# The products of an inverse 47-point unit, tied in issue order and begun on the second PSUM bank

## The chip, the cores and the metric

The kernel runs on one core of a Trainium2 chip. The metric is the device time of one execution in microseconds. Beside it stands a profile of one execution, taken on the chip. The engines are TensorE (PE, with its weight loads as PEld), VectorE (DVE), ScalarE (ACT), GpSimd (POOL) and SyncE (SP, which issues most DMAs).

## The reference

A filter along the sequence (a real Fourier transform, a complex mixing matrix, a soft threshold, the inverse transform) on 8 batches of 3008 positions and 256 channels, and behind it a gated feed-forward network (FFN) on all 24064 tokens:

```python
X = np.fft.rfft(x, axis=1)
Yr = Xr @ w_r - Xi @ w_i + b_r
Yi = Xr @ w_i + Xi @ w_r + b_i
Yr = np.sign(Yr) * np.maximum(np.abs(Yr) - lam, 0.0)   # the same for Yi
y = np.fft.irfft(Yr + 1j * Yi, n=x.shape[1], axis=1)
gate = 1.0 / (1.0 + np.exp(-(y @ w_gate)))
out = (gate * (y @ w_val)) @ w_out
```

## The kernel before

3008 is 47 · 64, so each transform is done as products with a table of 47 points (step a) and tables of 64 points (step b). The program has three parts. First the transforms of the first batches run in blocks whose order is the code's own (`tc.manual_schedule()`). Then the FFN of the first 9 · 512 tokens (`ffn1`, `ffn2`) runs together with the transforms of the other batches; here a scheduler decides the order on each engine: it goes by the order in the code and takes another instruction first where it expects that one to be ready sooner. From about 1021 us on, the remaining tokens go through the FFN in another algorithm, with an order that is written out by hand (`ORDER`, `slot`).

The change touches two helpers of step a.

`products_a` does the forward 47-point products: four products for a pair of PSUM banks `pa`, in the code's order second bank first.

`inv_a(u)` does the inverse ones for a unit `u` of 2 · 4 · 47 positions. Its input `vf` comes from DRAM in `load_v`, which `move` issues as two DMAs on SP: rows 0 to 47 first, rows 64 to 111 second. They belong to the two halves `j` of the unit. Each half is 16 products of 48 rows by 64 channels by 47 points (fp32), over four `h`, two `ct` and two `e`. The half decides which 64 rows of the array a product uses, and `e` which 64 columns: four quarters. Half `j` writes bank `pa[j]` (named `pia` in the profile; the program numbers its tiles, so the second bank of a unit has the higher number). Behind the products ACT copies both banks: to `yf`, which SP stores in DRAM (`yd`) for the last part, or to `yth`/`carry` for the FFN of the middle part. The banks come from a ring of 6 that `pg` and `pv` of the FFN use too; `vf` has 2 buffers, and a third tile for some units near the end.

The loop over `j` is in the middle, so the code goes two products on the first bank, two on the second, and so on. There are 64 units. Around each stand, on PE, the FFN's products `pg` and `pv` (L474 to L476, 12 of them) and `po` (L502 to L504, 6 of them). Sigmoid (L480), product (L482), split into `hh` and `hl` (L490, L491) of the FFN run on ACT and DVE.

`hook` is a list that is filled while the FFN runs in the blocks of fixed order, and is cleared behind them (`hook.clear()`).

Of the kernel before, what the change touches and what calls it, by code (L numbers as in the profile page):

```python
# [19 lines left out]
R2, R1 = 47, 64  # L20
# [101 lines left out]
def tile_fft_mix_ffn(ctx: ExitStack, tc, x, w_r, w_i, b_r, b_i, w_one, w_out, mf, mi, mis, fa, fb, mf0, fa0, out):  # L122
    nc = tc.nc
# [29 lines left out]
    def bank(name, tag="ring", bufs=RING):  # L153
        return (psf if tag == "ring" else psl).tile([P, 512], F32, tag=tag, bufs=bufs, name=name)
# [10 lines left out]
    fb_sb = const.tile([P, 64], F32, name="fb_sb")  # L165
# [3 lines left out]
    fa_sb = const.tile([P, 64], F32, name="fa_sb")  # L169
# [32 lines left out]
    def load_a(b, h):  # L202
# [4 lines left out]
            move(nc.sync, xf, xv[b, h])  # L207
        held["x", b, h] = xf

    def products_a(xs, outs, copies):  # L210
        pa = [bank("pa") for _ in range(2)]
        xs = [t[:, 2 * c:2 * c + 2] if t.shape[1] == 4 else t for c, t in enumerate(xs)]
        for j in (1, 0):
            rows = slice(64 * j, 64 * j + R2)
            for c in (1, 0):
                nc.tensor.matmul(pa[j][64 * c:64 * c + 64], fa_sb[rows], xs[c][rows], start=True, stop=True)
        for copy, o, t in zip(copies, outs, pa):
            copy(o, t.rearrange("p (h c) -> p h c", h=2))

    def fwd_a(b, h):  # L220

        xf = held["x", b, h]
        if b == 0:
            for i, copy in enumerate((nc.scalar.copy, nc.vector.tensor_copy)):
                pa, xi = bank("pa")[:2 * NQ], xf[:2 * NQ, 2 * i:2 * i + 2]
                nc.tensor.matmul(pa, fa0_sb, xi, start=True, stop=True)
                copy(xi, pa.rearrange("p (h c) -> p h c", h=2))
            return
        products_a((xf, xf), (xf[:, 0:2], xf[:, 2:4]), (nc.scalar.copy, nc.vector.tensor_copy if b < 2 else nc.scalar.copy))
# [13 lines left out]
    def halves_a(b, u):  # L243

        xs = [held.pop(("xh", b, 2 * u + c)) for c in range(2)]
        az = [p2.tile([P, 2, D], F32, tag="st", bufs=NST, name="azh") for _ in range(2)]
        products_a(xs, az, (nc.scalar.copy, nc.scalar.copy))
        for j in range(2):
            move(nc.gpsimd, az[j], zv[b][u, :, :, 2 * j:2 * j + 2], True)
# [144 lines left out]
    def split_y(c, at, n, y):  # L394
        if c not in yts:
            yts[c] = [p3.tile([P, CT, CW], F32R, name=t) for t in ("yth", "ytl")]
        yh, yl = (t[:, :, at:at + n] for t in yts[c])
        nc.scalar.copy(yh, y)
        sub(yl, y, yh)

    def inv_a(u):
        vf = held.pop(("v", u))
        pa = [bank("pia")[:, :CT * UT].rearrange("p (c k) -> p c k", c=CT) for _ in range(2)]
        for h in range(4):
            for ct in range(CT):
                for j in range(2):
                    rows = slice(64 * j, 64 * j + NQ)
                    for e in range(2):
                        ch = ct * P + 64 * e
                        nc.tensor.matmul(pa[j][64 * e:64 * e + 64, ct, h * R2:(h + 1) * R2], vf[rows, h, ch:ch + 64],  # L410
                                         fb_sb[rows, :R2], start=True, stop=True)
        first = 2 * u * UT // CW
        for j, py in enumerate(pa):
            lo, k = (2 * u + j) * UT, 0
            while k < UT:
                at = lo + k
                c, place = divmod(at, CW)
                n = UT - k if at >= T0 else min(UT - k, CW - place)
                y = py[:, :, k:k + n]
                if at >= T0:  # L420
                    t = result("yf")[:, :CT * n].rearrange("p (c k) -> p c k", c=CT)
                    nc.scalar.copy(t, y)
                    nc.sync.dma_start(yd[:, :, at - T0:at - T0 + n], t)
                elif c == first:
                    split_y(c, place, n, y)
                else:
                    if place == 0:
                        held["carry", c] = p3.tile([P, CT, 384], F32, name="carry", bufs=1), 0
                    t = held["carry", c][0]
                    nc.scalar.copy(t[:, :, place:place + n], y)  # L430
                    held["carry", c] = t, place + n
                k += n

    def result(name):
        return p3.tile([P, CW], F32, tag="ry", bufs=NYF, name=name)
# [11 lines left out]
    hook = []  # L447
# [111 lines left out]
    def ffn_units():  # L559
        units, todo = [], {}  # L560
        seq = [(c, f) for c in range(NPL) for f in range(NF)]

        def own(c):

            return range(-(-c * CW // (2 * UT)), -(-(c + 1) * CW // (2 * UT)))

        for c in range(1, NPL):
            at = (c - 1) * NF
            for i, u in enumerate(own(c)):
                todo.setdefault(at + (0, 4)[i], []).append(lambda u=u: load_v(u))  # L570
                todo.setdefault(at + (4, 8)[i], []).append(lambda u=u: inv_a(u))
            todo.setdefault(at + 1, []).append(lambda c=c: carry(c))

        def unit(n):
            c, f = seq[n]
            if n == 0:
                for i, u in enumerate(own(0)):
                    if i == 0:
                        w = w1h[:, 0].rearrange("p i t n -> p (i t n)")
                        keep_warm(bank("warm"), w[:, :P], w, WARM_V)  # L580
                    inv_a(u)
                ops("sum word", 0)
            ffn1(c, f)
            for t in todo.pop(n, ()):
                t()
            if n >= LAG and n - LAG < len(seq) - BEHIND:
                ffn2(*seq[n - LAG])
        return [lambda n=n: unit(n) for n in range(len(seq))], own(0), own(NPL - 1)[-1] + 1
# [61 lines left out]
    xs = {}  # L650
# [468 lines left out]
    def inverse(g):  # L1119

        us = [u for b in g for u in range(b * NV, (b + 1) * NV) if u >= u0]
        last = g == groups[-1]
        ahead = min(NVF - 1, len(us))
        todo = list(range(len(us)))

        def load(upto):
            while todo and todo[0] < upto:
                i = todo.pop(0)
                load_v(us[i], last and i > 4 and i % 3 == 2)

        def begin():
            load(ahead)

        def go(i):
            load(i + 1 + ahead + (last and i > 3))
            inv_a(us[i])
        return [(0.0, begin)], [(1.0, lambda i=i: go(i)) for i in range(len(us))]
# [32 lines left out]
    for j in range(NF, len(ffn)):  # L1170
        c, f = divmod(j, NF)
# [94 lines left out]
```

## Time and profile before

| what | before |
|---|---|
| median of 3 runs (lowest to highest) | 2664.31 us (2664.19 to 2669.71) |
| the profiled execution | 2665.18 us |
| its span, first to last instruction | 2663.2 us |
| granted TensorE clock, mean | 0.996 |
| PE busy | 2627.3 us (99%) |
| PEld busy | 2456.9 us (92%) |
| DVE, ACT, POOL busy | 1941.7, 1816.8, 1094.1 us |
| products of `pia` (records of PE) | 4096, from 99.8 to 1008.1 us |

A row of the timeline is the start in us, the time from the start to the end of the last instruction in it, the engine, the source line, the operation, what it writes and reads, the shape and the count; instructions of one kind that follow each other are one row. An fp32 product leaves two records, so a unit of `pia` counts x64. In brackets stands how long the engine was idle ahead of it, and what ended that.

### The profile page before, as it was taken

The numbers are of one execution on the slowest core, as the hardware profiler recorded it, in microseconds if no ns is written. First come the engines' busy times: TensorE is split into PE (matmuls) and PEld (weight loads), VectorE is DVE, ScalarE is ACT, GpSimd is POOL, SyncE is SP. The second block draws the span as 40 slices with busy tenths as digits, with TensorE's granted clock in tenths as the row PEclk, the third lists the DMA queues.
The fourth block names the chain that finished last, engine by engine and source line by source line (L and its number), as shares of the span: only waits on it lengthen the run. The fifth ranks groups of instructions, "written<-read, shape, count | busy, mean of one in ns | idle before, by whom it ended". The sixth has DMA issues, their size and how long they took to land. (4 is left out here: it accounts for less than half of the span.)

```text
span 2663.2 us, 60273 instructions
## 1 busy us (share of the span) xinstructions
PE 2627.3 (99%) x24032; PEld 2456.9 (92%) x24032; DVE 1941.7 (73%) x3468; ACT 1816.8 (68%) x3530; POOL 1094.1 (41%) x1399
## 2 busy tenths in 40 slices
PE   8999999999999999999999999999999999999998
PEld 6668888888899878999999999999999999999998
DVE  4768778777777525777777777777777777777777
ACT  4666655656565435777777777777777777777776
POOL 0241031123500002555555555555555555555554
PEclk9999999999999999999999999999999999999999
DMA  9887655777655572111111211111111211111111
GB/s 282 259 249 201 189 153 170 195 226 221 198 161 150 175 222 76 33 41 34 39 41 35 47 32 42 33 41 34 40 41 33 46 31 45 33 41 33 40 41 27
DMA packets 200969, 268.27 MB, mean 101 GB/s; under 512 B 19760, under 2 KB 152368, under 8 KB 200688
## 3 DMA queue, kind: packets, MB, share of 16 engines
q1 hardware_dynamic: 179600, 220.04, 28.1%
q0 software_dynamic: 20832, 44.31, 7.8%
q8 instruction: 189, 3.10, 0.5%
q14 instruction: 92, 0.75, 0.1%
q10 hardware_dynamic: 256, 0.07, 0.0%
HBM read 137.33 MB, written 127.01 MB: 99 GB/s over the span
## 5 line engine op out<-in xcount | busy, mean ns | idle before, releaser
L764 POOL TENSOR_TENSOR hs<-gh,xh 128x256 f32<-128x256 f32 x227 | 253.1, 1115 | 734.6 <-DVE gh L754 734.6
L754 DVE TENSOR_TENSOR gh<-gh,pa 128x256 f32<-128x256 f32 x228 | 96.1, 421 | 344.4 <-ACT gh L749 344.4
L713 PE MATMUL pd<-xop,th 128*128 128x256 f32 x1824 | 333.0, 276 | 0.8 <-DVE pc L757 0.8
L713 PE MATMUL pa<-xop,w1h 128*128 128x256 f32 x1824 | 332.6, 276 | 0.0
L713 PEld LDWEIGHTS pd<-xop,th 128*128 128x128 f32 x1824 | 274.5, 188 | 1.7 <-DVE pc L757 1.4
L713 PEld LDWEIGHTS pa<-xop,w1h 128*128 128x128 f32 x1824 | 274.6, 188 | 0.1
L713 PE MATMUL pd<-xop,tl 128*128 128x256 f32 x912 | 251.8, 276 | 0.0
L713 PE MATMUL pa<-xop,w1l 128*128 128x256 f32 x912 | 251.7, 276 | 0.0
L784 DVE TENSOR_TENSOR hpS<-hs,hpS 128x768 fp32r<-128x768 f32 x228 | 217.1, 952 | 0.4 <-ACT hpS L780 0.4
L733 ACT COPY pd<-pb 128x512 f32<-128x512 f32 x228 | 130.0, 570 | 107.8 <-PE pb L713 107.8
L757 DVE TENSOR_TENSOR pb<-pb,m 128x512 f32<-128x512 f32 x228 | 159.5, 699 | 42.3 <-PE pb L713 42.3
L327 PE MATMUL pm<-w_sb,xsh 128*128 128x256 f32 x1008 | 185.9, 286 | 4.1 <-ACT xsh L310 3.1
L780 ACT CAST hpS<-hs 128x768 fp32r<-128x768 f32 x228 | 189.5, 831 | 0.2 <-DVE hs L770 0.2
L729 PE MATMUL acc<-hpS,w2h 128*128 128x256 f32 x912 | 177.5, 276 | 0.0
L733 ACT COPY pb<-pa 128x512 f32<-128x512 f32 x228 | 130.0, 570 | 68.1 <-PE pa L713 68.0
L770 POOL TENSOR_TENSOR hs<-xh,hs 128x256 f32<-128x256 f32 x227 | 168.0, 740 | 17.8
L768 POOL TENSOR_TENSOR gh<-gh 128x256 f32<-128x256 f32 x227 | 167.3, 737 | 17.8
L713 PEld LDWEIGHTS pd<-xop,tl 128*128 128x128 f32 x912 | 171.2, 188 | 0.0
L713 PEld LDWEIGHTS pa<-xop,w1l 128*128 128x128 f32 x912 | 171.2, 188 | 0.0
L766 POOL TENSOR_TENSOR hs<-hs,gh 128x256 f32<-128x256 f32 x227 | 168.1, 741 | 0.0
L713 PE MATMUL pb<-xop,th 128*128 128x256 f32 x912 | 166.5, 276 | 0.0
L713 PE MATMUL pb<-xop,w1h 128*128 128x256 f32 x912 | 166.4, 276 | 0.0
(218 smaller groups left out, 8738.4 us busy)
## 6 DMA issues: line engine op xcount, KB each, us to landing
zf<-zd SPq DMA_DIRECT2D x96, 256.0 KB, 4.3
vf<-vd SPq DMA_DIRECT2D x128, 192.0 KB, 4.1
vd<-vz SPq DMA_DIRECT2D x85, 256.0 KB, 3.1
ypair<-yd SPq DMA_DIRECT2D x38, 512.0 KB, 3.6
yd<-yf SPq DMA_DIRECT2D x103, 188.0 KB, 3.8
out_dram<-ev SPq DMA_DIRECT2D x149, 128.0 KB, 1.8
out_dram<-ev POOLq DMA_DIRECT2D x37, 512.0 KB, 5.8
xf<-in_x_dram SPq DMA_DIRECT2D x80, 192.0 KB, 4.4
```

Source lines behind the costliest of these rows:

```text
L327: nc.tensor.matmul(o, l, r, start=(i == 0), stop=(i == len(mms) - 1))
L713: nc.tensor.matmul(o[:, i * HW:(i + 1) * HW], l, r, start=start, stop=l is wl, skip_group_check=True)
L729: nc.tensor.matmul(o, l, r, start=(p, b) not in begun, stop=l is wl, skip_group_check=True)
L733: nc.scalar.copy(to, o)
L754: nc.vector.tensor_mul(g, g, o[:, HW:])
L757: nc.vector.tensor_add(to, o, hx[k, "m5"])
L764: e.tensor_add(hx[k, "S"][:, 0], g[:, 1], x[:, 1])
L766: e.tensor_sub(hx[k, "S"][:, 1], hx[k, "S"][:, 0], g[:, 0])
L768: e.tensor_sub(g[:, 1], g[:, 0], g[:, 1])
L770: e.tensor_sub(hx[k, "S"][:, 2], x[:, 0], hx[k, "S"][:, 1])
L780: nc.scalar.copy(t[:, 0], parts_of(k, what))
L784: sub(t[:, 1], parts_of(k, what), t[:, 0])
```

## The change

A new helper `behind_last_of` ties each product to the instruction traced last on TensorE, from the second product of a unit on: the scheduler may not issue it ahead of that one. It is not a wait for the other to finish; it binds the order of issue alone, and other instructions may come between. In the blocks of fixed order (while `hook` is filled) no tie is made. `products_a` and `inv_a` use it, and the loop over `j` in `inv_a` runs from the second half to the first.

```diff
+    def behind_last_of(row, ins):
+        if row and not hook:
+            tc.keep_in_program_order(ins)
+        row.append(ins)
+
     def products_a(xs, outs, copies):
...
+        row = []
         for j in (1, 0):
             rows = slice(64 * j, 64 * j + R2)
             for c in (1, 0):
-                nc.tensor.matmul(pa[j][64 * c:64 * c + 64], fa_sb[rows], xs[c][rows], start=True, stop=True)
+                behind_last_of(row, nc.tensor.matmul(pa[j][64 * c:64 * c + 64], fa_sb[rows], xs[c][rows], start=True, stop=True))
...
     def inv_a(u):
...
+        row = []
         for h in range(4):
             for ct in range(CT):
-                for j in range(2):
+                for j in (1, 0):
                     rows = slice(64 * j, 64 * j + NQ)
                     for e in range(2):
                         ch = ct * P + 64 * e
-                        nc.tensor.matmul(pa[j][64 * e:64 * e + 64, ct, h * R2:(h + 1) * R2], vf[rows, h, ch:ch + 64],
-                                         fb_sb[rows, :R2], start=True, stop=True)
+                        o = pa[j][64 * e:64 * e + 64, ct, h * R2:(h + 1) * R2]
+                        behind_last_of(row, nc.tensor.matmul(o, vf[rows, h, ch:ch + 64], fb_sb[rows, :R2], start=True, stop=True))
```

What the scheduler makes of it on PE is shown at three places. The lines of the changed program are numbered 7 higher there (L410 is L417 or L418). First, before, a unit of the middle part (input `vf_11796`, banks `pia_11873` and `pia_11874`), in the stretch where the last transforms run beside the FFN:

```order
L503 MATMUL po_11411<-hh_11715,w2l_81 128x512
L504 MATMUL po_11411<-hl_11716,w2h_78 128x512
L410 MATMUL pia_11873<-fb_sb_79,vf_11796 64x47 x14
L410 MATMUL pia_11874<-fb_sb_79,vf_11796 64x47 x14
L410 MATMUL pia_11873<-fb_sb_79,vf_11796 64x47 x2
L410 MATMUL pia_11874<-fb_sb_79,vf_11796 64x47 x2
L474 MATMUL pg_11913<-yth_9588,w1h_77 128x512
```

The same unit in the changed program, its first rows:

```order
L509 MATMUL po_11410<-hh_11786,w2h_78 128x512
L510 MATMUL po_11410<-hh_11786,w2l_81 128x512
L511 MATMUL po_11410<-hl_11787,w2h_78 128x512
L509 MATMUL po_11411<-hh_11786,w2h_78 128x512
L418 MATMUL pia_11874<-fb_sb_79,vf_11796 64x47 x2
L418 MATMUL pia_11873<-fb_sb_79,vf_11796 64x47 x2
```

Fourteen products of one bank stood ahead of fourteen of the other; now two of the second bank and two of the first take turns, 16 rows in all, and four `po` products of the next step have moved ahead of the unit. Second, the unit behind it on PE before (input `vf_11870`), which was in two pieces:

```order
L504 MATMUL po_11411<-hl_11861,w2h_78 128x512
L410 MATMUL pia_11943<-fb_sb_79,vf_11870 64x47 x16
L502 MATMUL po_11410<-hh_11930,w2h_78 128x512
L503 MATMUL po_11410<-hh_11930,w2l_81 128x512
L504 MATMUL po_11410<-hl_11931,w2h_78 128x512
L410 MATMUL pia_11944<-fb_sb_79,vf_11870 64x47 x16
L474 MATMUL pg_11987<-yth_9588,w1h_77 128x512
```

and in the changed program:

```order
L509 MATMUL po_11410<-hh_11930,w2h_78 128x512
L510 MATMUL po_11410<-hh_11930,w2l_81 128x512
L511 MATMUL po_11410<-hl_11931,w2h_78 128x512
L509 MATMUL po_11411<-hh_11930,w2h_78 128x512
L510 MATMUL po_11411<-hh_11930,w2l_81 128x512
L511 MATMUL po_11411<-hl_11931,w2h_78 128x512
L418 MATMUL pia_11944<-fb_sb_79,vf_11870 64x47 x2
L418 MATMUL pia_11943<-fb_sb_79,vf_11870 64x47 x2
```

The two halves were 16 products of one bank, three `po` products, and 16 of the other; now the unit is one piece, with turns as above, behind the `po` products. Ten of the 64 units stood in one of these two forms before (five with the halves one behind the other, five in two pieces); the other 54 took turns, and still do, now second bank first. Third, the one unit (input `vf_12347`) that in the changed program has something in its midst, behind its first 24 products:

```order
L418 MATMUL pia_12506<-fb_sb_79,vf_12347 64x47 x2
L509 MATMUL po_12496<-hh_12337,w2h_78 128x512
L510 MATMUL po_12496<-hh_12337,w2l_81 128x512
L511 MATMUL po_12496<-hl_12338,w2h_78 128x512
L418 MATMUL pia_12507<-fb_sb_79,vf_12347 64x47 x2
```

Three `po` products that stood among the next `pg` products before stand between its third and its last quarter now. Elsewhere on PE nothing has moved but the `po` products next to these units. On ACT the copies of the two banks of some units have changed places, and in some units an FFN copy stands between them; on DVE three rows, on SP four loads and stores have changed places with their neighbours; POOL's list is the same.

## The prediction

> **What bounds the kernel now.** I read three views in this order: the busy time in two stretches of the span, the waits of TensorE in the first of them, and the end of the chain that finished last. In the first view the columns after the length are the busy time of PE, PEld, DVE, ACT and POOL, the granted clock, the share of the DMA engines and GB/s.
>
> ```profile
> 900.00:1010.00 110.00, 106.79 (x1542) 85.89 (x1542) 28.98 (x43) 41.67 (x84) 3.22 (x4) 1.00 0.77 217
> 1010.00:2663.00 1653.00, 1644.58 (x14428) 1640.28 (x14426) 1240.85 (x2290) 1240.42 (x2511) 898.58 (x1094) 1.00 0.16 38
> ...
> PE pia L410 <- DMA vf<-vd: 1.5, 1, 1.5
> PE po L502 <- ACT hh L490: 1.0, 1, 1.0
> PE pi L372 <- ACT yh L339: 0.4, 1, 0.4
> PE pi L373 <- DVE yl L340: 0.3, 1, 0.3
> ...
> 2655.69 0.52 PE acc L729 x2
> 2656.22 0.60 ACT ev L798
> ```
>
> TensorE is busy for 106.79 of 110 us in the stretch from 900 to 1010 us, and for 1644.58 of 1653 us behind it, to the last product 7 us ahead of the end. In the first stretch ACT (41.67) and DVE (28.98) have room; the DMA engines (0.77) have less. The four waits of PE there sum to 3.2 us, which is the whole of 110.00 − 106.79. So a microsecond less work for PE in this stretch starts everything behind it a microsecond earlier, unless one of these waits grows. The granted clock is 1.00 in both rows: no clock term.
>
> **What the order of a unit costs now.** The changed products are those of `pia`, L410: 64 units of 32 fp32 products, each product two records. The lists of instructions show three forms of a unit before. In 54 units the four quarters of the array take turns: two products into the first bank (rows 0–47), two into the second (rows 64–111). In five units all or most of one bank's products stand ahead of the other's. In five more the two halves are 16 products each, with other products between them. These ten lie between 918 and 998 us. The timeline of PE has all three forms; first a unit with turns:
>
> ```profile
> 962.61 0.39 PE L504 MATMUL po<-hl,w2h 128*128 128x512 f32 x1
> 962.93 1.15 PE L410 MATMUL pia<-fb_sb,vf 48*64 48x47 f32 x64
> 964.01 0.50 PE L474 MATMUL pg<-yth,w1h 128*128 128x512 f32 x1
> 964.34 0.40 PE L475 MATMUL pg<-ytl,w1h 128*128 128x512 f32 x1
> ```
>
> 64 records pass in 1.15 us. From the start of the product ahead (962.61) to that of the second one behind (964.34) are 1.73 us; two 512-column products without a unit between them start 0.23 apart (967.53 and 967.75 below are such a pair), so two steps would be 0.46, and the unit costs 1.27 us. Now the five in which the halves stand one behind the other:
>
> ```profile
> 918.56 1.75 PE L410 MATMUL pia<-fb_sb,vf 48*64 48x47 f32 x64
> ...
> 946.41 1.63 PE L410 MATMUL pia<-fb_sb,vf 48*64 48x47 f32 x64
> ...
> 956.94 1.75 PE L410 MATMUL pia<-fb_sb,vf 48*64 48x47 f32 x64
> ...
> 985.70 1.94 PE L410 MATMUL pia<-fb_sb,vf 48*64 48x47 f32 x64
> ...
> 990.51 1.75 PE L410 MATMUL pia<-fb_sb,vf 48*64 48x47 f32 x64
> ```
>
> The same 64 records, but only one half of the array's rows has work at a time. Over 1.15 they cost 0.60 + 0.48 + 0.60 + 0.79 + 0.60 = 3.07 us. The third form:
>
> ```profile
> 925.88 1.14 PE L410 MATMUL pia<-fb_sb,vf 48*64 48x47 f32 x32
> ...
> 940.43 1.14 PE L410 MATMUL pia<-fb_sb,vf 48*64 48x47 f32 x32 [1.47 <-DMA vf<-vd]
> ...
> 967.53 0.39 PE L502 MATMUL po<-hh,w2h 128*128 128x512 f32 x1
> 967.75 0.39 PE L503 MATMUL po<-hh,w2l 128*128 128x512 f32 x1
> 968.07 1.14 PE L410 MATMUL pia<-fb_sb,vf 48*64 48x47 f32 x32
> 969.14 0.50 PE L504 MATMUL po<-hl,w2h 128*128 128x512 f32 x1
> 969.47 0.40 PE L502 MATMUL po<-hh,w2h 128*128 128x512 f32 x1
> 969.71 0.39 PE L503 MATMUL po<-hh,w2l 128*128 128x512 f32 x1
> 970.03 1.13 PE L410 MATMUL pia<-fb_sb,vf 48*64 48x47 f32 x32
> 971.09 0.50 PE L474 MATMUL pg<-yth,w1h 128*128 128x512 f32 x1
> 971.43 0.40 PE L475 MATMUL pg<-ytl,w1h 128*128 128x512 f32 x1
> ...
> 976.33 1.14 PE L410 MATMUL pia<-fb_sb,vf 48*64 48x47 f32 x32
> ...
> 995.37 1.14 PE L410 MATMUL pia<-fb_sb,vf 48*64 48x47 f32 x32
> ```
>
> 32 records alone take as long as 64 with turns. From 967.75 to 969.47 are 1.72 us, less 0.46 is 1.26; from 969.71 to 971.43 again. The unit costs 2.52 where one with turns costs 1.27: 1.25 us too much, five times, is 6.25.
>
> **The change part by part.** (1) The ties in `products_a` move nothing: its products stand in the same places in both programs. Cost 0. (2) In `inv_a` every unit now takes turns, second bank first. So the five grouped units lose 3.07 us and the five divided ones 6.25. (3) One division is new: in the unit that runs at 968 us before, three `po` products now stand behind its first 24. A second block costs what a unit costs beyond its steady run: the records of a unit start within 1.15 − 0.23 = 0.92 us (0.23 is the median of one record, quoted below), so 1.27 − 0.92 = 0.35 us back. (4) In the other 54 units the sequence is the same ring of quarters, entered two places later. What changes is the quarter at the entry and at the exit. The divided unit shows both: its first half begins and ends on the first bank, the second half on the second bank. Entry: 967.75 to 968.07 and 969.71 to 970.03, 0.32 each. Exit, from the half's start to the next product: 1.07 and 1.06. Equal to 0.01, so 0 ± 0.01 × 64 = ±0.6 us. (5) The first product now waits for the second half of the unit's input, whose DMA is issued behind the first, and for the second bank; before, the third product did so. The trace has few such waits:
>
> ```profile
> L410 PE MATMUL pia<-fb_sb,vf x4096: 203/232/337, 99.8 to 1008.1; 48*64 48x47 f32 x196
> ...
> DMA vf<-vd: 2.2, 3
> ```
>
> Three waits for the input in the whole program. The two halves are issued within 0.9 us (990.05 below, two issues), so each of the three grows by 0.45 at the most: 0 to 1.3, taken as 0.2, near the lower end because the third product stood right behind the first two and met the same wait. (6) ACT's and DVE's lists change by swapped copies of the two banks; in the last stage one `xop` cast moves ahead of a `yf` copy and a sigmoid. Its input comes from POOL:
>
> ```profile
> 970.38 1.05 POOL L673 TENSOR_TENSOR ypair<-ypair 128x256 f32<-128x256 f32 x1
> ...
> 973.48 0.60 ACT L480 ACTIVATE sg<-pg 128x512 f32<-128x512 f32 x1 [3.67 <-PE pg L476]
> ```
>
> POOL is done at 971.43, and a cast of about 0.6 and a copy of 0.5 end near 972.5, while the sigmoid waits for PE until 973.48: 0, covered by 1 us; without that cover up to 1.1 us.
>
> (7) What comes late next are the loads of `vf`. The stretch has 17 units; the same bytes must come in about 101 us instead of 110, a DMA share of 0.77 × 110/101 = 0.84.
>
> ```profile
> DMA to landing us min/median/max: 3.2/5.0/8.2
> ...
> 990.05 0.88 SPq L186 DMA_DIRECT2D vf<-vd  x2
> ```
>
> The load issued at 990.05 belongs to the unit at 995.37: 5.3 us for a landing of 5.0 at the median. Between the two lies the unit at 990.51, which gets 0.60 shorter, so PE would wait 0.3 us there. Queued behind such a wait on PE are the next `pg` products, and ACT and DVE behind them. I take 0.3 for this place and nothing for the others, whose loads stand 6 to 10 us ahead; the bounds are −1.5 (the wait at 940.43 goes away) and 3.5 (several loads late).
>
> Sum: −3.07 − 6.25 + 0.35 + 0.2 + 0.3 = **−8.5 us**. The profiled execution took 2665.18 us (its span is 2663.2, 2.0 lie around it), so it would take 2656.7; it stands 0.9 above the median of the runs, 2664.31, which gives 2655.8. I forecast **2656**.
>
> [...]
>
> **The rivals.** *A, the forecast:* PE bounds the stretch and the gain reaches the end, 2654.5 to 2658. For it: the waits of 3.2 us in 110. Chance 0.70. *B, the loads take part of it back:* if five loads come 0.7 us late (between 0.3 and the 3.2 that separate the median landing from the longest), 3.5 us return: 2660, with a spread of 1.5 to both sides, so that some 45% of it is still faster by 0.2%. For it: the DMA share of 0.84, and SP, which issues loads and stores in one order. Against it: one such wait so far. Chance 0.20. *C, the change doesn't do what it says:* a unit that begins on the second bank doesn't run the quarters together, as if the order had no effect, and only four divisions at 0.35 go: −1.4, so 2663. [...] Against it: all 54 units with turns run at 1.15 or near it. Chance 0.05. *D, slower:* the first product of every unit waits for the second half of the input. It decides from a mean wait of 8.5/64 = 0.13 us, where the gain is gone; at 0.3 us a unit, two thirds of the 0.45 between the two issues, it is 64 × 0.3 − 8.5 = +10.7, so 2675. For it: the halves do land one behind the other. Against it: only three units wait for input at all. Chance 0.05.
>
> **How the numbers follow.** A measurement of this kernel tells about 0.2% (5.3 us) from no change, so faster means below 2659.0 and slower above 2669.6. Faster: A (0.70) less a little, and not quite half of B: 0.78. Same: the rest of B and C: 0.17. Slower: D: 0.05. The range takes in all of A with its bounds (−9.6 with nothing given back and the entries at their best, −1.5 more if the wait at 940.43 goes: 2653.2) and most of B: 2653 to 2661. C, D and the end of B stay out.
>
> **What would show it.** In the profile after, every `pia` row of the timeline between 900 and 1000 us should read x64 (or x128) with about 1.15 us, apart from one of x48 and one of x16; the last `pia` should start near 998.5 instead of 1007.2; PE's busy time from the first `acc` on should not change. A wait of PE for `vf` above 2 us in sum in that stretch means B. Units of 1.6 us or more mean C; waits ahead of most units mean D. I would be wrong if the stretch behind the FFN began with a wait for weights or `ypair` that is hidden now.

## The result, and the profile after

| | before | after |
|---|---|---|
| first series, 4 executions each: median | 2665.28 us | 2687.24 us |
| lowest to highest | 2664.19 to 2669.71 | 2683.24 to 2689.70 |
| the profiled execution, its span | 2665.18, 2663.2 | 2689.70, 2687.6 |
| granted TensorE clock, mean | 0.996 | 0.994 |

The ratio is 1.0083, with a 95% interval of 1.007 to 1.0096: slower by 0.8%, where 2656 was forecast. Three later series with the same changed kernel on three chips (12 executions each, below) gave 1.0000 (0.9972 to 1.0027), 1.0004 (0.999 to 1.0018) and 1.0000 (0.9988 to 1.0013); which chip the first series ran on is not on record. So two things have to be explained: why there is no gain of 8.5 us, and why the first series was 22 us slower. The ratios leave out the executions of 2700 us and more, which the kernel before (24 of 108) and most of the kernels below have now and then.

**The units took the form that was forecast.** The timeline of TensorE after, rows of `pia` (start, time, count):

```profile
918.22 1.15 PE L418 MATMUL pia<-fb_sb,vf 48*64 48x47 f32 x64
925.68 1.15 PE L418 MATMUL pia<-fb_sb,vf 48*64 48x47 f32 x64
929.70 2.08 PE L418 MATMUL pia<-fb_sb,vf 48*64 48x47 f32 x128
...
969.72 0.91 PE L418 MATMUL pia<-fb_sb,vf 48*64 48x47 f32 x48
971.46 0.45 PE L418 MATMUL pia<-fb_sb,vf 48*64 48x47 f32 x16
...
1003.74 1.15 PE L418 MATMUL pia<-fb_sb,vf 48*64 48x47 f32 x64
```

All units are whole, at 1.15 us, but one of x48 and x16. Yet the last one starts at 1003.74 where 998.5 was forecast, and the first product of the last stage at 1017.72, only 3.4 us ahead of the 1021.13 of before. Of these 3.4 us the change made 2.0: the unit that starts at 906.45 before, ahead of all ten that were in pieces or grouped, starts at 905.02 after, and in two runs in which these ten are as before (2 and 6 below) it starts at 903.98 and 904.21, so that such a difference comes from one execution to the next.

**Where the rest of the 9 us went.** First a stretch of 15 us (columns as in the prediction) and a row of the view of waits (us in sum, times, longest) before:

```profile
935.00:950.00 15.00, 13.53 (x170) 10.85 (x169) 2.76 (x4) 5.24 (x12) 0.00 (x0) 1.00 0.92 228
```

```profile
ACT yf L422 <- DMA yd<-yf: 6.0, 3, 3.0
```

and after:

```profile
935.00:950.00 15.00, 11.66 (x154) 8.76 (x154) 2.24 (x4) 3.40 (x7) 0.00 (x0) 0.77 0.81 206
```

```profile
ACT yf L429 <- DMA yd<-yf: 6.7, 4, 4.2
PE po L509 <- ACT hh L497: 4.7, 3, 3.3
```

PE waits 3.3 us at one place for `hh` (1.0 was the longest before), and the granted clock is 0.77 in that stretch, not 1.00: 15 × 0.23 = 3.4 us. TensorE there, after:

```profile
935.72 0.39 PE L511 MATMUL po<-hl,w2h 128*128 128x512 f32 x1
939.45 0.50 PE L509 MATMUL po<-hh,w2h 128*128 128x512 f32 x1 [3.34 <-ACT hh L497]
...
941.32 1.96 PE L418 MATMUL pia<-fb_sb,vf 48*64 48x47 f32 x64
943.21 0.79 PE L481 MATMUL pg<-yth,w1h 128*128 128x512 f32 x1
943.81 0.63 PE L482 MATMUL pg<-ytl,w1h 128*128 128x512 f32 x1
```

Behind the wait a 512-column product takes 0.63 us, not 0.39, and a unit 1.96, not 1.15; from 941 to 947 us the granted clock is 0.50. And VectorE and ScalarE there, after, and the same two rows of ScalarE before:

```profile
934.86 0.69 DVE L489 TENSOR_TENSOR sg<-sg,pv 128x512 f32<-128x512 f32 x1 [2.28 <-PE pv L483]
```

```profile
938.41 0.47 ACT L429 COPY yf<-pia 128x376 f32<-128x376 f32 x1 [4.23 <-DMA yd<-yf]
938.78 0.62 ACT L497 CAST hh<-sg 128x512 fp32r<-128x512 f32 x1
```

```profile
938.69 0.47 ACT L422 COPY yf<-pia 128x376 f32<-128x376 f32 x1 [2.37 <-DMA yd<-yf]
939.05 0.62 ACT L490 CAST hh<-sg 128x512 fp32r<-128x512 f32 x1
```

The reader is to see a queue. The copy to `yf` waits until one of three `yf` buffers has been stored in `yd`, 4.23 us; the cast to `hh`, for which TensorE waits, stands behind that copy in ScalarE's list and begins behind it, at 938.78, although its input `sg` is ready at 935.55. Before, the same two stood there at nearly the same time, but TensorE reached `hh` later: it had half of a divided unit ahead of it, and waited 1.47 us for that unit's `vf` instead. TensorE now comes earlier; the store does not.

From the start of the unit at 906.45 (905.02 after) to the first product of the last stage 114.67 us have become 112.71. By the starts of the products the units take 7.4 us less (27.6, now 20.2), and would take 8.2 less but for the one at half clock (1.96 instead of 1.15), where 9.0 was forecast. The waits of PE take 2.2 us more (5.4 us in the stretch from 900 us on, of it 4.7 for `hh`, where 3.2 stood). The products `pg`, `pv` and `po`, as many as before, take 3.2 us more. −7.4 + 2.2 + 3.2 = −2.0. The 3.2 and the 0.8 of the one unit are 4.0, of which the clock explains 3.4.

**What the last stage lost.** It has the same instructions in the same order, and TensorE is busy throughout. The windows, PE alone (length, busy, products in it, granted clock), before:

```profile
1320.00:1650.00 330.00, 330.00 (x2914) 1.00 0.16 37
1670.00:1990.00 320.00, 320.00 (x2826) 1.00 0.16 37
```

and after:

```profile
1100.00:1290.00 190.00, 190.00 (x1679) 1.00 0.15 35
1320.00:1650.00 330.00, 330.00 (x2804) 1.00 0.15 36
1670.00:1990.00 320.00, 320.00 (x2826) 1.00 0.16 36
2010.00:2350.00 340.00, 340.00 (x2889) 1.00 0.16 37
2370.00:2650.00 280.00, 280.00 (x2473) 1.00 0.15 35
```

330 us / 2914 is 113.2 ns a product, 330 / 2804 is 117.7: two paces, at the same granted clock of 1.00. A slot (one turn of the stage's loop) is 63 products. The slow pace holds in two stretches of exactly 48 slots (39 to 87 and 135 to 183), 3024 products × 4.5 ns = 13.6 us each; with the stalls below, the last stage is 27.8 us longer, and −3.4 + 27.8 = +24.4 is the difference of the two spans. At each of the four ends stands a small stall. TensorE at the first, after:

```profile
1300.12 0.28 PE L736 MATMUL acc<-hpX,w2l 128*128 128x256 f32 x1
1300.36 0.50 PE L720 MATMUL pb<-xop,w1h 128*128 128x256 f32 x2
```

and ScalarE, after, and in the same slot before:

```profile
1298.39 0.59 ACT L744 COPY m<-pc 128x512 f32<-128x512 f32 x1
1299.74 0.57 ACT L740 COPY pd<-pb 128x512 f32<-128x512 f32 x1 [0.76 <-PE pb L720]
```

```profile
1301.84 0.59 ACT L737 COPY m<-pc 128x512 f32<-128x512 f32 x1
1302.90 0.57 ACT L733 COPY pd<-pb 128x512 f32<-128x512 f32 x1 [0.48 <-PE pb L713]
```

The product that overwrites `pb` starts 0.24 us behind the one ahead, not 0.11, since ScalarE copies `pb` 0.28 us late (0.76 of idle time instead of 0.48). The product of `pb` that it waits for is not late: the copy starts 0.64 us behind the start of that product (1299.10), where it was 0.35 before.

What tells these slots from others is the place of that copy in ScalarE's list of instructions in the compiled program, counted from 0 with its semaphore waits: at slots 39, 87, 135 and 183 it is number 64 modulo 128. A slot has about 13 instructions, and 48 slots have 640, five times 128. Before, the copy is never at 64: ScalarE's whole list has 4536 instructions before and 4507 after, because the new order ahead of the last stage needs fewer waits. The page has a queue named `instruction` with 92 packets of 8.2 KB. The lists of ScalarE, VectorE, GpSimd and SyncE after have 11846 instructions together, which is 92.5 blocks of 128; that a packet holds one such block is an estimate from these two numbers. The page, and the DMA view from 1300.4 to 1300.6 us:

```profile
q14 instruction: 92, 0.75, 0.1%
```

```profile
q14 instruction: 1, 0.01, 13.1%
```

This packet starts at 1300.44, 0.70 us behind the start of the late copy. In all seven profiles with such stalls, 32 stalls in all, a packet of this queue starts 0.64 to 0.70 us behind the late copy. The author reads it as a sign that a block changes there; but the copy does not wait for that packet, which comes behind it, and what takes the 0.28 us is not shown.

So the theory (1), to be tested: where a block of 128 begins with this copy, the fetch (the change of blocks) makes the copy 0.28 us late and TensorE stalls by 0.13; and a stall can leave the train of products at another pace. The rivals: the changed transforms or the chip make the pace (2), or only the fetch does (3).

### The profile page after: what moved, and what is told of

Read it like the earlier page. It is cut to its first block, busy times and chain, and to the rows that moved or that the text cites. A ratio compares the mean times of both kernels' runs of the same rounds, so it can differ in the third digit from the quotient of the medians.

```text
span 2687.6 us, 60232 instructions
## 1 busy us (share of the span) xinstructions
PE 2648.9 (99%) x24032; PEld 2477.3 (92%) x24032; DVE 1942.9 (72%) x3468; ACT 1817.5 (68%) x3530; POOL 1091.7 (41%) x1399
## 5 line engine op out<-in xcount | busy, mean ns | idle before, releaser
L720 PE MATMUL pc<-xop,w1h 128*128 128x256 f32 x912 | 168.6, 278 | 0.0
```

The costliest lines, as they stand in the source:

```text
L720: nc.tensor.matmul(o[:, i * HW:(i + 1) * HW], l, r, start=start, stop=l is wl, skip_group_check=True)
```

## The experiments

| run | time, median of the executions below 2700 us | before, same chip | ratio (95%) |
|---|---|---|---|
| after, two copies more | 2659.23 | 2663.89 | 0.9975 (0.9964 to 0.9986) |
| before, one copy more | 2667.77 | 2663.89 | 1.0022 (0.9992 to 1.0051) |
| ties alone | 2659.71 | 2663.89 | 0.9976 (0.9964 to 0.9988) |
| reversal alone | 2660.95 | 2663.89 | 0.9987 (0.9974 to 1.0001) |
| after, second series | 2660.04 | 2663.40 | 1.0000 (0.9972 to 1.0027) |
| before, copy behind a sigmoid | 2673.75 | 2663.40 | 1.0063 (1.0019 to 1.0106) |
| four `yf`, three `vz` | 2660.17 | 2663.40 | 0.9991 (0.9981 to 1.0001) |
| four `yf`, four `f2k` | 2656.37 | 2663.40 | 0.9971 (0.9961 to 0.9981) |
| after, third series | 2662.20 | 2663.66 | 1.0004 (0.999 to 1.0018) |
| after, one copy more | 2660.02 | 2663.66 | 0.9989 (0.9979 to 0.9998) |
| four `yf`, four `f2k`, again | 2655.62 | 2663.66 | 0.9970 (0.9959 to 0.9981) |
| after, fourth series | 2663.27 | 2664.02 | 1.0000 (0.9988 to 1.0013) |

**1. The changed kernel, ScalarE's list moved by two.** The edit, ahead of the last stage:

```diff
     with tc.manual_schedule():
+        for i in range(2):
+            nc.scalar.copy(both[:, 2 + i:3 + i], lam_sb)
         for k in range(NU - min(off for _, off in ORDER)):
```

> The changed kernel with two tiny copies (128x1) more on ScalarE, issued between the last transform and the first slot of the last stage. They move every later ScalarE instruction two places on in its list and touch nothing ahead of 1010 us. In the changed kernel the list index of the copy of pd (L740) is 64 modulo 128 at slots 39, 87, 135 and 183, which are the four places where PE stalls and its pace changes; with two more it is 64 at no slot. Theory 1 (ScalarE takes its instructions in blocks of 128; where a new block begins with this copy the copy is late, PE stalls, and PE's train of products then runs at 117.8 instead of 113.3 ns until the next such stall): no stall above 200 ns and no slow stretch in the last stage, time 2660 to 2663 us, that is 24 to 29 below the changed kernel. Rival 2 (the slow pace comes from the changed transforms ahead, for instance from the later phase in which the last stage is entered, or from the chip in this execution): the slow stretches stay, about 2687 us, perhaps at other slots.

The windows of this run:

```profile
1320.00:1630.00 310.00, 310.00 (x2738) 1.00 0.16 37
```

The products go at 113.2 ns, no stall above 135 ns stands between slots 2 and 227, and the ratio is 0.9975. Two instructions of 128 × 1 are all that differs from the changed kernel. That the stalls go with them is as theory 1 has it. The fast pace alone would not tell theory 1 from rival 2, for the changed kernel runs at that pace too in the later series (5, 9, 12).

**2. The kernel before, moved by one.** The same edit with `range(1)`.

> The kernel before with one tiny copy (128x1) more on ScalarE at the same place. In the kernel before the copy of pd never has index 64 modulo 128; with one more it has at slots 8, 37, 56, 85, 104, 133, 152, 181 and 200. Theory 1: stalls of PE of about 0.1 us at these nine slots, and the pace changes at each: slow in 8 to 37, 56 to 85, 104 to 133, 152 to 181 and 200 to 228, which is 144 slots of 63 products at 4.5 ns more, +41 us, and +1 for the stalls, so about 2706 us; if the pace doesn't start from fast, the other slots, 76 of 228, are slow and it is about 2687. Theory 1b (the late copies stall PE but the pace is something else): 2665 to 2666. Rival 2: no change, 2664.

All nine stalls stand at the nine forecast slots, and none elsewhere. ScalarE at slot 104, and the windows from slot 85 on:

```profile
1767.01 0.59 ACT L737 COPY m<-pc 128x512 f32<-128x512 f32 x1
1768.37 0.57 ACT L733 COPY pd<-pb 128x512 f32<-128x512 f32 x1 [0.77 <-PE pb L713]
```

```profile
1640.00:1760.00 120.00, 120.00 (x1061) 1.00 0.17 40
1780.00:1980.00 200.00, 200.00 (x1700) 1.00 0.16 38
2000.00:2120.00 120.00, 120.00 (x1021) 1.00 0.16 36
2140.00:2320.00 180.00, 180.00 (x1590) 1.00 0.17 39
2340.00:2460.00 120.00, 120.00 (x1021) 1.00 0.17 40
```

113.1, then 117.6 and 117.5, then 113.2, then 117.5. The pace changed at three of the nine, slots 104, 152 and 181: 95 slow slots, +27 us, and this execution took 2693.88. The other nine took 2662 to 2684. So a stall's place follows from the list; whether the pace changes there does not. That part of theory 1 (a change at each stall) was wrong.

**3 and 4. The two parts of the change, each alone** (the ties with `for j in range(2)`; the loop `for j in (1, 0)` without ties).

> The ties alone, with the loop over the halves in the old order (first bank first). Every unit should still be one piece with turns. ScalarE's list has the length of the kernel before (4536), so that the copy of pd is at index 64 modulo 128 nowhere. Theory 1: the last stage as in the kernel before, and the time is that of the stretch up to 1020 us alone: between 2655 (all of the 9 us of the units) and 2661 (3.4 us, as in the changed kernel). Rival 2 in the form that the ties or the shorter units make the slow pace: about 2687.

> The reversed loop alone (second bank first), no ties. Units in pieces and with the halves grouped may remain. ScalarE's list has 4507 instructions as in the changed kernel, with the copy of pd at index 64 modulo 128 at slots 39, 87, 135 and 183. Theory 1: the four stalls and the two slow stretches of 48 slots are there, +27 us in the last stage: 2683 to 2692 us, whatever the units gain or lose. Rival 2 in the form that the ties make the slow pace: 2660 to 2668.

The ties alone keep the list at 4536, have no stall in the last stage and gain 0.24%. In their profile TensorE waits for `vf` near 936 us (2.5 us), not for `hh`. The reversal alone has 4507, and its profile shows the four stalls at slots 39, 87, 135 and 183 (starts 0.24 to 0.25 apart), but the fast pace all through, and 2658.25 us. So the reversal is what shortens the list, the stalls come with it, and a stall alone costs only its 0.13 us. The expected +27 did not come.

**5, 9 and 12. The changed kernel again, three series.** The program is the one of the result.

> The changed kernel as it is, on another chip than at first. The runs so far show the four stalls (slots 39, 87, 135, 183) with the reversal alone too, and there the pace did not change at any of them. So theory 1 now reads: the late copy of pd only gives PE a stall, and a stall can move PE's train from the pace of 113.3 to that of 117.8 ns and back, or leave it; which of these depends on fractions of a clock. Then the executions lie in steps of 13.5 us (48 slots of 63 products at 4.5 ns) above some 2659 us: 2659, 2672 to 2674, 2686 to 2688, with a share of them whole steps up. Rival 2 (the changed program always runs at the slow pace in slots 39 to 87 and 135 to 183): all executions at 2683 to 2690 as at first.

> The changed kernel once more, in another series. At first it took 2683 to 2690 us in 4 of 4 executions, in the second series 2654 to 2670 in 10 of 12 and 2691 and 2700 in two. Theory 1 with a pace that each stall redraws: most at 2654 to 2664 (no slow stretch), some one to three stretches of 13.5 us above, none near 2725 (slow from the first slot to the last), since four stalls give it four chances to come back. If which pace a stall leaves is a property of the chip and not of the single execution, the executions of this series agree with one another, on 2660 or on 2687.

> The changed kernel a last time, for how often it runs as in the first series (2683 to 2690 us in 4 of 4). In the two later series 4 of 24 executions were above 2672. If every stall redraws the pace by itself, a fifth or so of the executions of this series is above 2672 and the others lie at 2654 to 2669; none is near 2725. If it is a property of the chip or of the state it is in, this series agrees with itself, at 2660 or at 2687.

In each profile the four stalls are at their slots; in none does the pace change. TensorE at slot 39 in the third series, and a window behind it:

```profile
1296.41 0.28 PE L736 MATMUL acc<-hpX,w2l 128*128 128x256 f32 x1
1296.65 0.50 PE L720 MATMUL pb<-xop,w1h 128*128 128x256 f32 x2
```

```profile
1320.00:1630.00 310.00, 310.00 (x2738) 1.00 0.16 37
```

The same stall of 0.24 as in the first series, and 113.2 ns behind it. Of these 36 executions 30 took 2653.7 to 2669.8, and six 2672.5, 2675.4, 2676.5, 2691.1, 2700.2 and 2702.8 (the last two stand outside the ratios). The kernel before has none between 2671 and 2716 in 108. The four of the first series are all in that gap, so the slow stretches are not fixed by the program. Six in 36 and four in four hardly have one chance in common; what the first series had of its own stays open. On what it depends whether a stall changes the pace, no run shows; the fractions of a clock of the expectation were the author's guess.

**6. A late copy away from number 64.** In eleven slots of the kernel before, 20 to 220, the copy of `pd` stands behind the sigmoid `g11`:

```diff
-        for name, off in ORDER:
+        order = list(ORDER)
+        if k in range(20, 221, 20):
+            i = order.index(("seedd", 0))
+            order.insert(i + 2, order.pop(i))
+        for name, off in order:
```

> The kernel before, in which the copy of pd stands behind the sigmoid g11 on ScalarE instead of ahead of it, in the eleven slots 20, 40, ... 220; nothing else is changed. The sigmoid takes 0.31 us of ScalarE, about as much as a copy is late in the slots where a block of 128 begins with it (0.28). Each swap also adds one instruction to the list, so that index 64 falls on the copy at slots 37, 75 and 209 besides. Theory 1 (a stall of PE at this place is what changes the pace, whatever makes the copy late): a stall of 0.1 to 0.2 us at each of the eleven slots and at 37, 75 and 209, changes of pace at some of these fourteen slots and nowhere else; time between 2666 and 2730 us. Rival 3 (only the fetch of a block does it): stalls at the eleven slots without a change of pace, changes only at 37, 75 or 209. Rival 4 (pace has nothing to do with stalls): changes at other slots.

TensorE at slot 20:

```profile
1166.98 0.28 PE L729 MATMUL acc<-hpX,w2l 128*128 128x256 f32 x1
1167.88 0.51 PE L713 MATMUL pb<-xop,w1h 128*128 128x256 f32 x2 [0.62 <-ACT pd L733]
```

The sigmoid waits for a later product (1.11 us of idle time ahead of it), so the stall was 0.79 us more than a step (0.90 − 0.11), not 0.1 to 0.2: eleven make 8.7, and the profile took 2675.26. Stalls of 0.24 stood at 37, 75 and 209, as the list says. The pace changed at none of the fourteen; of the four executions one took 2695.58. The run doesn't decide between theory 1 and rival 3.

**7, 8 and 11. A fourth buffer for `yf`.** With one tiny copy to keep the list off 64, and room taken from `st`, the buffers of `vz` (`NST` 4 to 3, run 7), or from `f2k` (`NF2K` 5 to 4, runs 8 and 11, whose edit this is):

```diff
-NF2K, NR2K, NLD, NST, NBIG, NMF, NME, NVF, NVO, NHH, NSG, NYF = 5, 4, 3, 4, 6, 3, 2, 2, 1, 3, 2, 3
+NF2K, NR2K, NLD, NST, NBIG, NMF, NME, NVF, NVO, NHH, NSG, NYF = 4, 4, 3, 4, 6, 3, 2, 2, 1, 3, 2, 4
```

> The changed kernel with 4 instead of 3 buffers for the yf and ot tiles, which ScalarE's copies of pia write; room for it is made by 3 instead of 4 buffers for the vz and azh tiles. One tiny copy on ScalarE keeps index 64 off the copy of pd in the last stage, as two did in the run with the changed kernel and two copies. Theory 5 (of the 9 us that the units give, 2.8 to 3.3 are lost because a copy to yf, which waits for a store of yd, stands ahead of the cast to hh on ScalarE, and 1.8 to 3.4 because the clock falls behind this idle time): the wait of PE for hh at 936 to 939 us goes from 2.9-3.3 to below 1 us, the clock stays at 1.00 there, the last stage begins 8 to 10 us behind the start of the last 100 us as measured from the unit at 900 us as against 4 us less than before, and the time is 2653 to 2656 us. Rival 6 (PE would wait for something else there, vf or pg): same wait under another name, 2659 to 2661. If fewer buffers for vz hurt, the time up to 900 us grows.

> The same with the room taken from the f2k tiles (4 instead of 5 buffers) and one tiny copy. Theory 5: 2653 to 2656 us; rival 6: 2659 to 2661; more, if the f2k tiles need their five buffers.

> The version with four buffers for yf and ot, four for f2k and one tiny copy, again, beside the changed kernel. Theory 5 and 1: 2653 to 2659 us, about 7 below the kernel before and 4 below the undisturbed executions of the changed kernel; in no execution one or two slow stretches, but some slow from the first slot to the last (2716 to 2726).

ScalarE in the last of these, and PE's waits there:

```profile
938.58 0.85 ACT L429 COPY yf<-pia 128x376 f32<-128x376 f32 x2 [6.07 <-PE pia L418]
943.30 0.62 ACT L497 CAST hh<-sg 128x512 fp32r<-128x512 f32 x1 [1.58 <-DVE sg L489]
```

```profile
PE pia L418 <- DMA vf<-vd: 2.4, 1, 2.4
PE po L509 <- ACT hh L497: 1.4, 2, 1.0
```

`yf` waits for its products, no longer for a store, and PE's wait for `hh` is 1.4 in sum, 1.0 at most, in all three runs. With three buffers it is 2.75 to 4.33 us at this place in all six profiles that have both parts of the change. So the store is shown to be what holds `hh` up. From the unit that starts at 906.45 before to the start of the last stage these three runs gain 5.3, 6.4 and 5.3 us on before; the eight profiles with three buffers (these six and runs 3 and 4) 1.0 to 5.3, 3.1 in the mean. On one chip the version took 2655.62 and the changed kernel with one tiny copy, equally free of stalls, 2660.02. The expected 8 to 10 did not come, for PE now waits 1.1 to 2.4 us for `vf`; nor did the expected clock of 1.00, which is 0.89 from 935 to 950 us in all three (15 × 0.11 = 1.7 us). With the room taken from `st` the time was 2660.17 where that from `f2k` gave 2656.37 on the same chip: the fourth buffer of `st` is worth its room. The version with `f2k` beats the kernel before by 0.3% twice, and the changed kernel on the same chips by 3.7 and 6.6 us.

**10. One copy more: number 64 is the wait ahead of the copy.**

> The changed kernel with one tiny copy more on ScalarE. Now the block of 128 begins with the wait ahead of the copy of pd (index 64) at slots 39, 87, 135 and 183, and the copy stands at 65. ScalarE is idle for 0.48 us at that wait in every slot. Theory 1: a delay of 0.28 us there is hidden by the idle time: no stall of PE, no change of pace, time as with two copies (2655 to 2664 us, apart from executions that are slow from the start). Rival 7 (the copy is late wherever a block begins near it): stalls at the four slots as in the changed kernel.

ScalarE at slot 39, and two windows:

```profile
1305.88 0.57 ACT L740 COPY pd<-pb 128x512 f32<-128x512 f32 x1 [0.52 <-PE pb L720]
```

```profile
1100.00:1290.00 190.00, 190.00 (x1616) 1.00 0.15 34
...
2370.00:2640.00 270.00, 270.00 (x2295) 1.00 0.16 36
```

There is no stall at any of the four slots: with the copy at number 65, ScalarE's idle time ahead of it is 0.52 us there, as in the other slots of this profile. This agrees with theory 1, by which the idle time hides the delay; the delay itself is in no row. Yet this profile, of an execution of 2720.99 us, shows the slow pace (117.6) from the third slot to the last, and so does that of run 7. The slow pace needs no late copy: here the products have it almost from the stage's start, and why is open.

Over all fourteen profiles there are 32 stalls with the copy at number 64 modulo 128, all where the list puts them. 27 met the fast pace, and 4 of these changed it to the slow one; 5 met the slow pace, and 3 of these changed it back. Between slots 2 and 227 the pace changed nowhere else.

## Why the prediction was wrong, point by point

- **What bounds the kernel.** "A microsecond less work for PE in this stretch starts everything behind it a microsecond earlier, unless one of these waits grows": right, and one of the four waits shown grew, that for `hh`, from 1.0 to 3.3. "No clock term" failed in this profile: behind that wait another 3.4 us were lost at half clock. Part of that differs from one execution to the next. In eleven of the fourteen profiles the granted clock falls to half near 940 us, for 3.4 or 6.8 us (from 925 to 950 us it is 0.93 in run 2 and 0.86 in the changed kernel), also in runs 2 and 6, where the ten units are as before. The length of the wait alone does not decide it: the fall comes behind 1.11 us in run 8 (the first two rows: a 512-column product takes 0.63 us) and does not come behind 2.95 us in run 10 (the other two: 0.39 us).

```profile
937.12 1.46 PE L418 MATMUL pia<-fb_sb,vf 48*64 48x47 f32 x64 [1.11 <-DMA vf<-vd]
939.50 0.63 PE L481 MATMUL pg<-yth,w1h 128*128 128x512 f32 x1
```

```profile
938.20 0.50 PE L509 MATMUL po<-hh,w2h 128*128 128x512 f32 x1 [2.95 <-ACT hh L497]
938.54 0.39 PE L510 MATMUL po<-hh,w2l 128*128 128x512 f32 x1
```

Falls also come behind waits of 2.46 us in run 3 and 2.75 in run 5; what decides it is not shown.

- **Steps (1) to (4)** held: all units whole at 1.15 us, but for one at half clock, and one divided. Their sum of 9.0 measured 8.2. Rival C fell: 64 starts again fit into a row of 1.15 us.
- **Step (5)** held: PE waits for `vf` nowhere in this stretch after (+0.2 taken); the 1.47 us of before went away, which was the lower bound of (7). Rival D, a wait ahead of every unit, fell: the kernel came out slower in the first series by another mechanism.
- **Step (7)** is the step that failed. "What comes late next are the loads of `vf`", at 0.3 us: late next was a store, `yd` from `yf`, which holds ScalarE's queue and through it `hh`. The row "ACT yf <- DMA yd<-yf: 6.0, 3, 3.0" was in the view of waits before, on an engine with 38% busy time, and was not followed to who stands behind it. In place of 0.3 with a bound of 3.5, the waits measured +2.2 and the clock +3.4 in this profile, and 0.6 stays unexplained. Rival B had the kind right, a transfer that gives part back, with the wrong transfer; that its 2660 is within 4 us of the later series (2660.0, 2662.2, 2663.3) is partly luck, since it holds neither the clock nor the slow stretches. With the ties alone (run 3) the wait was for `vf`, as step (7) has it, but 2.5 us long.
- **Step (6)** ("ACT's and DVE's lists change": 0) looked at which rows change places, not at the length of the list. That 29 fewer entries ahead of the last stage move the numbers of all later instructions, and 64 modulo 128 onto the one copy that PE waits for, at four slots, was nowhere in the sum, and "PE's busy time from the first `acc` on should not change" failed: +27.8 us in the first profile. The late copies are shown (runs 1, 2, 10); that a change of blocks makes them late is not: the author infers it from the 128 and from the packet behind each. That the pace changes at such stalls is shown for seven of 32; that a stall elsewhere suffices is not (none of eleven in run 6), and what made it change in the first series, and hardly in the later ones, is open.

## What to carry over

When a step gets shorter, look in the view of waits for every instruction that waits for a transfer, and ask what stands behind it in its engine's list and who waits for that; the wait that grows need not be TensorE's own in the profile before (here it was ScalarE's for a store, 2.37 us before and 4.23 after). In this kernel a loop of fixed order that runs TensorE without a gap got four stalls with 29 fewer instructions ahead of it in ScalarE's list, and lost them with two tiny copies more: compare the starts of equal products between two traces, slot by slot, before a cause is sought in what was changed. One series of four executions put this kernel at +0.8%, three series of twelve on three chips at 0.0%; the interval of one series does not cover that.

## What was not expected of the hardware

- In the last stage TensorE's 256-column products with a weight load each went at one of two paces, 113.2 ns (330 us / 2914, before) or 117.7 (330 / 2804, after), at a granted clock of 1.00, in run 10 the slow one from the third to the last of 228 slots. The pace changed at 7 of 32 short stalls; what makes the two is open.
- ScalarE's copy of `pd` started about 0.28 us late where it was number 64 modulo 128 of its list, 32 times of 32, and a packet of the instruction queue started 0.64 to 0.70 us behind it.
- The granted clock fell to half behind a wait of 1.11 us (run 8: 0.89 from 935 to 950 us, a 512-column product 0.63 us) and did not behind one of 2.95 us (run 10: 0.39).
